# Moving the first weight roundings of a fused attention and MLP kernel: later MLP roundings, a projection piece on VectorE, and three rounds of maxima taken forward

## The chip, the cores and the metric

The kernel runs on one core of a Trainium2 chip. A core has five engines with a queue of their own each: TensorE (PE; its weight loads are shown apart as PEld), VectorE (DVE), ScalarE (ACT), GpSimd (POOL) and SyncE (SP), which here issues nearly all DMAs. The metric is device time in microseconds (us), the median of several executions. All times below on the trace's own clock are us from the start of the profiled span.

## The reference

For x of 2048 tokens by 576 features, the reference gates an attention branch against an MLP branch:

```
g = sigmoid(sum(x * gate_w))                     # one gate per token
q, k, v = split(x @ wqkv)                        # 32 heads of 18 features
a = softmax(q k^T * 18**-0.5) v  @ wo
y = layernorm(x)
b = gelu(y @ w1 + b1) @ w2 + b2                  # 4608 hidden features
out = g * a + (1 - g) * b
```

All inputs and outputs are float32.

## The kernel before

Products are made with operands in a rounded 32-bit form. To keep float32 accuracy each operand is split into a rounded part and a remainder: an engine writes the rounded part (ACT, lines 370, 692, 710, 722, 777), another one subtracts it from the source (POOL or DVE, lines 166, 693, 711, 723, 778), and a product becomes three.

**Projection stage.** The first part of the program (lines 804 to 905) goes through four blocks of 512 tokens (`tb` 0 to 3). Each block has 17 groups `g`: nine of q and k (`qk_group`, 14 products of 512 columns each) and eight of v (`v_group`, 14 products of 288 columns). Between the groups the loop places other work by group number: the normalisation (`norm`, DVE, in block 3 at groups 2 to 5), the transposition of the normalised x (`y_chunk`: four TensorE transposes into a PSUM bank, ACT rounds it, DVE subtracts; in block 3 at groups 8 to 12), loads, and rounds of attention maxima.

**wqkv.** In block 0 the weights arrive in seven pieces (0 to 4 of q and k, 5 and 6 of v), through two buffers in turn. `W_AT` says at which group piece n is split (`split_w`: ACT rounds, the given engine subtracts) and piece n+2 loaded into the buffer that piece n leaves.

**Rounds of maxima.** Softmax takes the maximum of a row first. A round (`s1_round`) is two score products (line 210, one PSUM bank each) and two DVE maxima (line 212). The first unit (one pair of heads, half of the queries) has 32 rounds; `ROUNDS` says how many stand behind each group. When all 32 are done, `s1_finish` (lines 220 to 223, DVE), a transposition on TensorE (line 227), a copy on ACT (229) and two DMAs bring the maxima to the q operand. 40 rounds in all precede the main loop: those that the groups don't hold are made right after the last group, with one `run_due` each. In this stage all products of line 210, the transposes of x and line 227 share the three banks of `ps_s1` in turn, so the fourth waits until the first one's reader is done.

**MLP weights.** The MLP runs as a generator whose steps are interleaved with attention. Its w1 comes in pairs of chunks (one 576 KB load in two DMAs, line 349, into the one buffer `R1`), its w2 in single chunks (line 355, two buffers in turn). `split` puts a job in the list `bg`: ACT rounds (line 370), POOL subtracts (line 166), and then the next load into the buffer is issued. A job may run once the program's step counter `slot` has passed the number in `LOADED`, that is a fixed count of steps behind the load's issue. `run_due` makes such a step; in block 3 `SLOTS` calls it once per group up to group 8 and twice from group 9. The first loads stand at group 2, the first three jobs at group 9, and the second part of the normalised input (`load_y(0, 1)`, six DMAs of 384 KB, line 124) inside group 16, on the SP queue behind that group's store of v (line 802). Everything is recorded in this order, and each engine runs its own queue in order.

**Main loop.** 512 steps of score products (line 250), exponentials (ACT, 253), maxima of the next unit, products with v (268) and pieces of the MLP (454 first layer, 534 second layer). The first MLP products stand in step 1; the first pair has 18 products twice with the first part of the normalised input, and then 18 with its second part (six behind each third of the load).

Of the kernel before, what the change touches and what calls it, by code (L numbers as in the profile page):

```python
# [40 lines left out]
LAND = 8  # L41
# [5 lines left out]
LAST = 28  # L47
PSTEP = (489, 494, 497, 499)
ORDER = (0, 1, 3, 2)
ROUNDS = [lambda g: 0, lambda g: int(g >= 8), lambda g: int(g >= 2), lambda g: int(g >= 5)]  # L50
SLOTS = [lambda g: 0, lambda g: 0, lambda g: int(g >= 4), lambda g: 1 if g < 9 else 2]
SKIP = 0
N_AT = 5
W_AT = {0: 1, 1: 2, 2: 3, 4: 4, 6: 5, 8: 6}
W_CUT = (0, 128, 416, 704, 992, 2 * D, 3 * D - 288, 3 * D)
NSTEP = 512
FIN = NSTEP - 12
# [3 lines left out]
def gated_mix_kernel(ctx: ExitStack, tc: tile.TileContext, x, wqkv, wo, w1, b1, w2, b2, gate_w, out):  # L61
    nc = tc.nc
# [38 lines left out]
    def psum(pool):  # L101
        return pool.tile([P, TB], F32, name="ps")
# [16 lines left out]
    def bcast_rows(ap, n):  # L119
        return bass.AP(tensor=ap.tensor, offset=ap.offset, ap=[[0, P], [1, n]])  # L120
# [6 lines left out]
    slot = [0]  # L127
# [183 lines left out]
    looped = [False]  # L311
# [9 lines left out]
    def mlp():  # L321
# [3 lines left out]
        n = len(seq)  # L325
# [3 lines left out]
        def chunk(q):  # L329

            i, m = divmod(q, G // 2)
            return i, m, seq[i][1] * G + 2 * m
# [5 lines left out]
        LOADED = {}  # L338
        NQ0 = npair // NB

        def load_w1(q):

            if (1, q) in LOADED or q >= NQ0:
                return
            LOADED[1, q] = slot[0] + (LAND if looped[0] else 5)
            fc = chunk(q)[2]
            for h in range(2):
                src = w1[:, (fc + h) * P:(fc + h + 1) * P]
                nc.sync.dma_start(R1[64 * h:64 * h + 64], src.rearrange("(c p) n -> p c n", p=64))

        def load_w2(c):
            if (2, c) in LOADED or c >= NFC:
                return
            LOADED[2, c] = slot[0] + (LAND - 2 if looped[0] else 3)
            nc.sync.dma_start(R2[c % 2], w2[c * P:(c + 1) * P, :])

        def rounded(dst, src):
# [241 lines left out]
        for i in range(n + 1):  # L599
            q = 2 * i  # L600
# [49 lines left out]
    with ExitStack() as a:  # L650
# [17 lines left out]
        def load_x(tb):  # L668

            xt[tb] = x_tile()  # L670
            v = x_view(tb)
            rows = x[tb * TB:(tb + 1) * TB, :].rearrange("(t p) d -> p t d", p=P)
            for c0, c1 in ((0, 256), (256, D)) if tb == 0 else ((0, D),):
                nc.sync.dma_start(v[:, :, c0:c1], rows[:, :, c0:c1])
            nc.sync.dma_start(v[:, :, D:], rows[:, :, 512:D])
# [3 lines left out]
        def load_w(n):  # L679
            cs = slice(W_CUT[n], W_CUT[n + 1])  # L680
            wide = W_CUT[n + 1] - W_CUT[n]
            raw = pp.tile([P, 2, 2, TB], F32, name="p").rearrange("p a b c -> p (a b c)")[:, :5 * wide]
            raw = wraw[n] = raw.rearrange("p (c n) -> p c n", n=wide)
            nc.sync.dma_start(raw[:, 0:4, :], wqkv[0:512, cs].rearrange("(c p) n -> p c n", p=P))
            nc.sync.dma_start(raw[0:64, 4, :], wqkv[512:576, cs])
            nc.sync.dma_start(raw[64:128, 4, :], wqkv[512:576, cs])

        def split_w(n, eng):
            c0 = W_CUT[n] if W_CUT[n] < 2 * D else W_CUT[n] - 2 * D
            hi, lo = [w_[:, :, c0:c0 + W_CUT[n + 1] - W_CUT[n]] for w_ in (W_QK if W_CUT[n] < 2 * D else W_V)]  # L690
            raw = wraw.pop(n)
            nc.scalar.activation(hi, raw, AF.Copy)
            eng.tensor_tensor(lo, raw, hi.bitcast(F32), op=ALU.subtract)  # L693
# [38 lines left out]
        def norm(tb, stage):  # L732

            xv = x_view(tb)
            ts_ = slice(4 * tb, 4 * tb + 4)
            if stage < 2:
                for t in (2 * stage, 2 * stage + 1):
                    st6 = sm.tile([P, 2, nc.vector.BN_STATS_DIM], F32, name="st6")
                    for n in range(2):
                        nc.vector.bn_stats(st6[:, n, :], xv[:, t, n * ND:(n + 1) * ND])  # L740
                    nc.vector.bn_aggr(stats[:, tb * 4 + t, :], st6)
            if stage == 1:
                rstd = rstds[tb] = sm.tile([P, 4], F32, name="rstd")
                sd = sm.tile([P, 4], F32, name="sd")
                var = sm.tile([P, 4], F32, name="var")
                nc.vector.tensor_scalar(var, stats[:, ts_, 1], LN_EPS, None, op0=ALU.add)
                nc.scalar.activation(sd, var, AF.Sqrt)

                nc.vector.reciprocal(rstd, sd)
                nc.vector.tensor_mul(rstd, rstd, var)  # L750
                nc.vector.tensor_add(sd, sd, rstd)
                nc.vector.tensor_scalar(sd, sd, 0.5, None, op0=ALU.mult)
                nc.vector.reciprocal(rstd, sd)
            if stage >= 2:
                junk = pp.tile([P, 2, 2, TB], F32, name="p").rearrange("p a b c -> p (a b c)")
                for t in (2 * stage - 4, 2 * stage - 3):
                    tt = 4 * tb + t
                    nc.vector.scalar_tensor_tensor(junk[:, :D], xv[:, t, 0:D], 1.0, gwb, op0=ALU.mult, op1=ALU.mult,  # L758
                                                   accum_out=glog[:, tt:tt + 1])
                    nc.vector.tensor_scalar(xv[:, t, :], xv[:, t, :], stats[:, tt, 0:1], rstds[tb][:, t:t + 1],  # L760
                                            op0=ALU.subtract, op1=ALU.mult)
# [61 lines left out]
        for tb in range(NB):  # L823
            work = [(qk_group, (tb, mt)) for mt in (range(9) if tb < 2 else (4, 0, 1, 2, 3, 5, 6, 7, 8))] + [(v_group, (tb, t, n)) for t in range(4) for n in range(2)]
            for g, (fn, args) in enumerate(work):
                if tb == 0:
                    if g in W_AT:
                        n = W_AT[g]
                        split_w(n, nc.gpsimd if n > 1 else nc.vector)
                        if n + 2 < 7:  # L830
                            load_w(n + 2)
                    if g == 10:
                        nc.sync.dma_start(b2b, bcast_rows(b2, D))
                        nc.sync.dma_start(b1r, b1.rearrange("(c p) -> c p", p=P))
                if tb == NB - 1 and g == 16:
                    args += (lambda: next(stream[0]),)
                fn(*args)
                ng = g - (N_AT if tb == 0 else 2)
                if 0 <= ng < 4:
                    norm(tb, ng)  # L840
                if tb + 1 < NB and 2 <= g < 7:
                    x_chunk(tb + 1, g - 2)
                yg = g - (11 if tb == 0 else 8)
                if 0 <= yg < 5:
                    y_chunk(tb, yg)
                if g == (16 if tb == 0 else 13) and tb + 2 < NB:
                    load_x(tb + 2)
                if tb == NB - 1:
                    if g == 1:
                        load_k(0, 3 * TB, S)  # L850
                    if g == 2:
                        load_q(1)
                        next(stream[0])
                    if g == 9:
                        qkstack.close()
                        wp1 = mstack.enter_context(tc.tile_pool(name="m_w1", bufs=3))
                        wp2 = mstack.enter_context(tc.tile_pool(name="m_w2", bufs=4))
                        next(stream[0])

                        nc.scalar.activation(gate, glog, AF.Exp, scale=-1.0)  # L860
                    if g == 14:
                        nc.vector.tensor_scalar(gate, gate, 1.0, None, op0=ALU.add)
                        nc.vector.reciprocal(gate, gate)
                        nc.vector.tensor_scalar(gate1, gate, -1.0, 1.0, op0=ALU.mult, op1=ALU.add)
                    if g == 7:
                        ps = psum(ps_s1)
                        nc.tensor.transpose(ps[:, :NFC], b1r, ident[:NFC, :NFC])
                        nc.vector.tensor_copy(b1t, ps[:, :NFC])
                if tb == 1 and g == 5:
                    load_q(0)  # L870
                    load_k(0, 0, TB)
                if tb == 1 and g == 9:
                    load_k(0, TB, 2 * TB)
                if tb == 2 and g == 4:
                    load_k(0, 2 * TB, 3 * TB)
                for _ in range(ROUNDS[tb](g)):
                    next_round()
                for _ in range(SLOTS[tb](g)):
                    run_due()
# [282 lines left out]
```

## Time and profile before

| what | value |
|---|---|
| median of the runs | 2332.59 us (2330.83 to 2334.19, 3 runs) |
| the profiled execution | 2332.71 us |
| its span in the trace | 2330.9 us |
| TensorE busy | 2290.9 us, 98% |
| VectorE, ScalarE, GpSimd busy | 71%, 61%, 42% |
| granted TensorE clock, mean | 0.997 |

The profiled execution lies 0.12 us above the median, and 1.8 us of it lie outside the span. TensorE is busy nearly throughout, so time is lost or won where TensorE stands idle or has half its clock. The projection stage ends at about 244 us; the main loop follows up to about 2210 us, and the last projection behind it.

### The profile page before, as it was taken

The numbers are of one execution on the slowest core, as the hardware profiler recorded it, in microseconds if no ns is written. First come the engines' busy times: TensorE is split into PE (matmuls) and PEld (weight loads), VectorE is DVE, ScalarE is ACT, GpSimd is POOL, SyncE is SP. The second block draws the span as 40 slices with busy tenths as digits, with TensorE's granted clock in tenths as the row PEclk, the third lists the DMA queues.
The fourth block names the chain that finished last, engine by engine and source line by source line (L and its number), as shares of the span: only waits on it lengthen the run. The fifth ranks groups of instructions, "written<-read, shape, count | busy, mean of one in ns | idle before, by whom it ended". The sixth has DMA issues, their size and how long they took to land.

```text
span 2330.9 us, 51536 instructions
## 1 busy us (share of the span) xinstructions
PE 2290.9 (98%) x20585; PEld 1566.0 (67%) x20585; DVE 1654.7 (71%) x2890; ACT 1424.6 (61%) x2629; POOL 968.5 (42%) x965
## 2 busy tenths in 40 slices
PE   8998999999999999999999999999999999999999
PEld 7876666666666666666666666666666666666668
DVE  5675677777777777777777777777777777777734
ACT  4222567777676666666666666666666666666662
POOL 4001566666555433333353444444434333333700
PEclk9999899999999999999999999999999999999999
DMA  7747845445456523343263524242354233242264
GB/s 244 243 151 234 235 163 154 140 145 143 133 189 166 159 96 118 103 135 110 76 172 130 161 95 120 94 138 96 118 162 151 95 107 105 99 147 91 77 213 160
DMA packets 165022, 330.31 MB, mean 142 GB/s; under 512 B 57190, under 2 KB 84490, under 8 KB 154054
## 3 DMA queue, kind: packets, MB, share of 16 engines
q1 hardware_dynamic: 163162, 323.76, 44.2%
q8 instruction: 162, 2.65, 0.5%
q10 hardware_dynamic: 1620, 3.26, 0.4%
q14 instruction: 78, 0.64, 0.1%
HBM read 234.16 MB, written 96.58 MB: 142 GB/s over the span
## 4 chain that ended last, share of the span: by engine, by line
PE 93%; DVE 3%; issue 1%; DMA 1%; SPq 0%; ACT 0%; POOL 0%; ACTq 0%; DVEq 0%; POOLq 0%
PE ps L534 21%; PE ps L268 20%; PE ps L454 20%; PE ps L250 13%; PE ps L210 11%; PE ps L771 3%; PE ps L1058 3%; PE ps L792 2%; DVE m L212 1%; DMA p<-in_A_wqkv_dram 0%; PE ps L698 0%; DVE p L758 0%; DVE x L760 0%; DVE hl L778 0%; PE ps L227 0%
## 5 line engine op out<-in xcount | busy, mean ns | idle before, releaser
L212 DVE TENSOR_REDUCE m<-ps 128x1 f32<-128x512 f32 x2048 | 1317.0, 685 | 460.3 <-PE ps L210 442.8
L253 ACT ACTIVATE p<-ps 128x512 f32<-128x512 f32 x1368 | 742.0, 596 | 404.3 <-PE ps L250 393.0
L166 POOL TENSOR_SCALAR zz<-zz 128x512 f32<-128x512 f32 x288 | 178.5, 620 | 826.0 <-ACT zz L507 796.1
L454 PE MATMUL ps<-big,w 64*128 64x512 f32 x3888 | 513.5, 393 | 0.1
L534 PE MATMUL ps<-w,hh 64*128 64x288 f32 x4352 | 489.9, 299 | 12.5 <-ACT z L475 0.4
L253 ACT ACTIVATE ring<-ps 128x512 f32<-128x512 f32 x680 | 369.1, 596 | 203.0 <-PE ps L250 199.5
L210 PE MATMUL ps<-ka,qa 54*128 54x512 f32 x2048 | 454.6, 415 | 10.3 <-DVE hl L723 5.4
L250 PE MATMUL ps<-qa,ka 56*128 56x512 f32 x2048 | 453.6, 422 | 1.6 <-ACT p L253 1.0
L454 PEld LDWEIGHTS ps<-big,w 64*128 64x128 f32 x3888 | 381.0, 185 | 74.6 <-ACT z L475 0.4
L534 PEld LDWEIGHTS ps<-w,hh 64*128 64x128 f32 x4352 | 383.5, 185 | 68.4 <-issue 45.4
L166 POOL TENSOR_TENSOR zz<-zz,z 128x512 f32<-128x512 f32 x288 | 371.8, 1291 | 24.0
L250 PEld LDWEIGHTS ps<-qa,ka 56*128 56x128 f32 x2048 | 205.1, 184 | 215.1 <-DVE m L212 179.3
L268 PE MATMUL ps<-p,vt 128*32 128x512 f32 x2736 | 344.6, 598 | 0.0
L534 PE MATMUL ps<-w,hl 64*128 64x288 f32 x2176 | 334.2, 292 | 0.0
L210 PEld LDWEIGHTS ps<-ka,qa 54*128 54x128 f32 x2048 | 213.4, 186 | 79.5 <-ACT p L253 25.6
L166 POOL TENSOR_TENSOR w<-x,w 128x576 fp32r<-128x576 f32 (+1 forms) x54 | 98.5, 1839 | 306.1 <-ACT w L370 272.3
L534 PEld LDWEIGHTS ps<-w,hl 64*128 64x128 f32 x2176 | 218.1, 185 | 5.1
L166 POOL TENSOR_TENSOR hl<-zz,hh 128x512 fp32r<-128x512 f32 x136 | 176.7, 1299 | 11.3
L268 PE MATMUL ps<-ring,vt 128*32 128x512 f32 x1360 | 179.1, 598 | 0.0
L268 PEld LDWEIGHTS ps<-p,vt 128*32 128x32 f32 x2736 | 71.4, 109 | 159.4 <-issue 152.1
L543 DVE SCALAR_TENSOR_TENSOR x<-ps,x 128x288 f32<-128x288 f32 x256 | 104.1, 448 | 11.8 <-PE ps L534 11.8
L771 PE MATMUL ps<-big,wqk 128*128 128x512 f32 x432 | 109.7, 402 | 1.4 <-POOL wqk L693 1.4
(100 smaller groups left out, 1368.4 us busy)
## 6 DMA issues: line engine op xcount, KB each, us to landing
w<-w_scr SPq DMA_DIRECT2D x54, 1152.0 KB
w<-w_scr SPq DMA_DIRECT2D x108, 576.0 KB
x<-in_B_w_dram SPq DMA_DIRECT2D x72, 288.0 KB
w_scr<-w SPq DMA_DIRECT2D x18, 1152.0 KB
w_scr<-w SPq DMA_DIRECT2D x36, 576.0 KB
big<-y_scr SPq DMA_DIRECT2D x42, 384.0 KB
qa<-qk_scr SPq DMA_DIRECT2D x192, 72.0 KB
ka<-qk_scr SPq DMA_DIRECT2D x84, 144.0 KB
```

Source lines behind the costliest of these rows:

```text
L166: fn(*args, **kw)
L210: nc.tensor.matmul(ps, qa[r0:r0 + 54, t * P:(t + 1) * P], ka[r0:r0 + 54, kb * TB:(kb + 1) * TB], start=True, stop=True)
L212: nc.vector.tensor_reduce(M4[u][:, h, t, kb:kb + 1], ps, axis=AX.X, op=ALU.max)
L250: nc.tensor.matmul(ps[h], ka[r0:r0 + 56, kc * P:(kc + 1) * P], qa[r0:r0 + 56, qb * TB:(qb + 1) * TB], start=True, stop=True)
L253: nc.scalar.activation(RING[n % 3][:, qb, h], ps[h], AF.Exp, scale=SCALE)
L268: nc.tensor.matmul(OB[u][r:r + 32, :], v[:, k, 19 * h:19 * h + 32], RING[c % 3][:, qb, h, :], start=(k == 0), stop=(k == NT - 1))
L454: nc.tensor.matmul(ps[h], wt[w_][r, c, :], Y[s_][r, c, :], start=(k == 0), stop=(k == 26))
L534: nc.tensor.matmul(ps[nn][:, :ND], h_[r, tok], w_[p_][r, cs[nn]], start=(k == 0), stop=(k == 6 * G - 1))
L543: nc.vector.scalar_tensor_tensor(dst, ps[nn][:, :ND], 0.5, b2b[:, cs[nn]] if g == 0 else dst, op0=ALU.mult, op1=ALU.add)
L771: nc.tensor.matmul(ps, w_[:, c, ms], big[:, s_, :], start=(k == 0), stop=False)
L792: nc.tensor.matmul(ps[:, :ND], big[:, s_, tok], w_[:, c, cs], start=(k == 0), stop=False)
L1058: nc.tensor.matmul(ps[:, :ND], OT[b][2][:, s_, tok], w_part(w_, c)[:, cs], start=(k == 0), stop=(k == 13))
```

## The change

Five edits, all of them to constants that place work:

- `W_AT`: the first piece of v (5) is split at group 5 in place of 6, the second (6) at group 7 in place of 8; the loads that follow a split go with it.
- `split_w` of piece 2 subtracts on VectorE in place of GpSimd.
- `ROUNDS` of block 3: groups 5, 6 and 7 hold two rounds each in place of one, so three of the rounds that stood right before the main loop (four there) move forward. The 32nd round of the first unit then stands at group 9 in place of 12, and its `s1_finish` and the transposition of line 227 move with it, to groups 9 and 10 (line 227 stands right behind group 10's round).
- `LOADED` of w1 and w2 ahead of the main loop: 7 steps in place of 5 and 3.

```
-ROUNDS = [lambda g: 0, lambda g: int(g >= 8), lambda g: int(g >= 2), lambda g: int(g >= 5)]
+ROUNDS = [lambda g: 0, lambda g: int(g >= 8), lambda g: int(g >= 2), lambda g: int(g >= 5) + int(5 <= g < 8)]
...
-W_AT = {0: 1, 1: 2, 2: 3, 4: 4, 6: 5, 8: 6}
+W_AT = {0: 1, 1: 2, 2: 3, 4: 4, 5: 5, 7: 6}
...
-            LOADED[1, q] = slot[0] + (LAND if looped[0] else 5)
+            LOADED[1, q] = slot[0] + (LAND if looped[0] else 7)
...
-            LOADED[2, c] = slot[0] + (LAND - 2 if looped[0] else 3)
+            LOADED[2, c] = slot[0] + (LAND - 2 if looped[0] else 7)
...
-                        split_w(n, nc.gpsimd if n > 1 else nc.vector)
+                        split_w(n, nc.gpsimd if n > 2 else nc.vector)
```

What this does to the queues, engine by engine: the first three MLP roundings on ACT keep their place (group 9). Those of the third and fourth w2 chunk move from between the roundings of the fourth and fifth `y_chunk` to behind the ScalarE copy of group 13's v, where that of the second w1 pair follows them; the third w1 pair's rounding moves from just before the main loop's first exponentials to behind the first four of them. On SP, the load of the third w1 pair still stands one place ahead of group 16's store of v and of `load_y(0, 1)`, and it waits for the subtraction of the second pair, which now comes later; the loads of q and k for the next units move ahead of the first store of a split weight. From the loop's first tens of steps on, the order of the instructions is the same on every engine.

## The prediction

> **What bounds the kernel now.** I read the page first, then windows, then the timelines of the stage that the edits touch.
>
> ```profile
> span 2330.9 us, 51536 instructions
> PE 93%; DVE 3%; issue 1%; DMA 1%; SPq 0%; ACT 0%; POOL 0%; ACTq 0%; DVEq 0%; POOLq 0%
> ```
>
> The chain of waits is 93% TensorE, so the change is worth the idle or half-clock time of TensorE that it takes away, less what it adds. Windows show where that is (columns: length, then busy time of PE, PEld, DVE, ACT, POOL, each with its count, then the granted clock, DMA share, GB/s):
>
> ```profile
> 20.00:40.00 20.00, 18.59 (x91) 14.88 (x90) 9.75 (x22) 9.66 (x13) 11.06 (x4) 1.00 0.83 244
> 220.00:240.00 20.00, 14.03 (x75) 11.26 (x74) 8.85 (x19) 5.00 (x10) 9.82 (x6) 0.83 0.70 233
> 229.20:232.60 3.40, 0.00 (x0) 0.00 (x0) 0.00 (x0) 1.20 (x3) 1.81 (x2) 1.00 0.99 326
> 232.60:239.40 6.80, 5.50 (x19) 4.26 (x19) 4.05 (x10) 1.59 (x3) 3.24 (x2) 0.50 0.51 171
> 246.30:249.70 3.40, 2.79 (x7) 1.02 (x6) 3.40 (x7) 0.40 (x1) 2.62 (x1) 1.00 1.02 259
> 249.70:256.50 6.80, 6.80 (x28) 5.74 (x30) 3.61 (x6) 2.27 (x4) 0.00 (x0) 0.50 1.07 217
> 242.00:244.00 2.00, 2.00 (x16) 1.88 (x14) 1.29 (x2) 0.24 (x1) 0.00 (x0) 1.00 1.13 242
> 247.00:257.00 10.00, 9.50 (x38) 7.08 (x39) 6.36 (x12) 2.47 (x5) 2.40 (x1) 0.66 1.06 225
> ```
>
> TensorE is nearly full except around 228 to 233, and its clock is halved twice, for 6.8 us each: after it stood idle, and after a stretch (246.3 to 249.7) of seven products only. An episode costs at most 6.8 / 2 = 3.4 us.
>
> **Step 1, the front.** Piece 2 and the v pieces end two waits.
>
> ```profile
> 22.64 2.60 PE L771 MATMUL ps<-big,wqk 128*128 128x512 f32 x10 [1.41 <-POOL wqk L693]
> 46.85 1.71 PE L792 MATMUL ps<-wv,big 128*128 128x288 f32 x11 [1.05 <-POOL wv L693]
> 17.76 1.41 ACT L692 ACTIVATE wqk<-p 128x1440 fp32r<-128x1440 f32 x1 [3.54 <-DMA p<-in_A_wqkv_dram]
> 12.28 1.66 DVE L693 TENSOR_TENSOR wqk<-p,wqk 128x1440 fp32r<-128x1440 f32 x1 [0.65 <-ACT wqk L692]
> 41.39 0.58 ACT L777 ACTIVATE hh<-ps 128x512 fp32r<-128x512 f32 x1
> ```
>
> Piece 2 is rounded at 19.2; a subtraction of its size takes 1.66 on DVE, so it is there at 20.9, before TensorE asks at 21.2: -1.4. On DVE the splits of groups 1 and 2 queue behind it, 1.7 us later at most, and behind those only SP's stores of q and k; no product waits for them, so this costs nothing while the buffers of those splits (six) last. SP's load of piece 4 waits for this subtraction and goes out sooner, and POOL has one job less. The last v piece's rounding now stands ahead of the copy at 41.39, 0.5 sooner; its chain and TensorE both shift by the 1.4, so the 1.05 wait shrinks by 0.5. Sum -1.9 (bounds -1.4 and -2.5, both waits gone).
>
> **Step 2, two rounds behind groups 5 to 7.** This is the change's price.
>
> ```profile
> 198.11 0.50 PE L210 MATMUL ps<-ka,qa 54*128 54x512 f32 x2
> 198.55 3.06 PE L771 MATMUL ps<-big,wqk 128*128 128x512 f32 x12
> 202.77 1.28 DVE L212 TENSOR_REDUCE m<-ps 128x1 f32<-128x512 f32 x2
> 203.51 0.50 PE L210 MATMUL ps<-ka,qa 54*128 54x512 f32 x1 [1.00 <-DVE m L212]
> 203.94 3.07 PE L771 MATMUL ps<-big,wqk 128*128 128x512 f32 x12
> 207.08 0.39 PE L774 MATMUL ps<-big,wqk 128*128 128x512 f32 x1
> 207.90 3.06 PE L771 MATMUL ps<-big,wqk 128*128 128x512 f32 x12
> 208.90 1.28 DVE L212 TENSOR_REDUCE m<-ps 128x1 f32<-128x512 f32 x2
> ```
>
> DVE is in the normalisation until 202.8. The first maximum ends at 203.4, and the fourth product since 198.1 (now group 6's second) waits for it to 203.51. With four products behind group 5 the fourth is theirs: TensorE idles from about 199.0 (three products of 0.22 and their drain) to 203.5. Queued behind it are group 6's fourteen products, and behind those ScalarE's copy, DVE's split and two stores on SP. Group 6 starts at 203.94, not 198.55: +5.4. Behind groups 6 and 7 the fourth product waits for that group's split and one maximum: from the end at 207.4 to 208.90 + 0.64 is 2.1, against about 0.9 for three products, 1.2 idle each. Group 8 starts at 203.94 + 2 x (3.45 + 2.1 + 0.2) = 215.4, not 207.90: +7.5. If DVE's normalisation were done sooner the 5.4 would shrink to the 1.2 of the others; nothing in the edits moves it, so the bounds are +5 and +8.
>
> **Step 3, the clock after that gap.** 4.5 us of idle stand between the two known cases, idle from 227.9 to 233.35 and the seven-product stretch, which both halved the clock. Half clock for 6.8 us falls on the one dense group of 3.4 us, which then takes up to twice as long, and partly on the next 1.2 wait, which hides some: I take +2.6, near the 5.50 busy us of 232.6 to 239.4, half of which was lost (2.75). Bounds 0 (no halving) and 3.4.
>
> **Step 4, line 227 earlier.** It takes the bank of the third normalised chunk, whose rounding stands behind the first MLP jobs.
>
> ```profile
> 215.00 0.66 PE L698 MATMUL ps<-ident,x 128*128 128x128 f32 x4 [0.65 <-DVE hl L723]
> 217.72 2.29 ACT L370 ACTIVATE w<-x 128x1152 fp32r<-128x1152 f32 x3
> 220.53 0.69 DVE L723 TENSOR_TENSOR hl<-ps,hh 128x512 fp32r<-128x512 f32 x1 [1.31 <-ACT hh L722]
> 222.01 0.97 PE L210 MATMUL ps<-ka,qa 54*128 54x512 f32 x2
> ```
>
> That bank is free 6.3 us behind the second chunk's transposes (215.0 to 221.2); TensorE would be there after 3.9: +2.35. Gone are the 0.65, about 0.6 in the round behind it, and 0.45 at 222.01, which came of a late ScalarE. Net +0.6 (bounds -1.7 and +2.4). Queued behind line 227 is group 11. The finish's four small DVE instructions, the copy on ScalarE and two DMAs on SP move too; the DMAs now stand ahead of the fourth w2 chunk's load and delay it by their issue, which step 5's later rounding covers.
>
> **Step 5, the roundings behind their loads.**
>
> ```profile
> 228.42 0.68 ACT L370 ACTIVATE w<-x 128x576 fp32r<-128x576 f32 x1 [5.70 <-DMA x<-in_B_w_dram]
> 231.40 0.68 ACT L370 ACTIVATE w<-x 128x576 fp32r<-128x576 f32 x1 [2.30 <-DMA x<-in_B_w_dram]
> 233.35 1.39 PE L210 MATMUL ps<-ka,qa 54*128 54x512 f32 x2 [5.41 <-DVE hl L723]
> 235.29 0.39 PE L227 MATMUL ps<-ident,nm 128*32 128x128 f32 x1 [0.56 <-DVE nm L223]
> ```
>
> ScalarE stood at two roundings for their loads, with the last chunk's rounding queued behind, for whose bank TensorE waited. These now stand behind group 13's copy, with no bank of TensorE behind them. So 5.4 and line 227's 0.6 go, and with the idle window the first half-clock stretch: half of its 5.50 busy us, 2.7. Sum -8.7 (bounds -6, the stretch staying, and -8.7).
>
> **Step 6, the rounds ahead of the loop.**
>
> ```profile
> 244.13 0.73 PE L210 MATMUL ps<-ka,qa 54*128 54x512 f32 x3
> 245.41 4.09 PE L210 MATMUL ps<-ka,qa 54*128 54x512 f32 x7 [0.55 <-DVE m L212]
> 249.59 1.39 PE L250 MATMUL ps<-qa,ka 56*128 56x512 f32 x2
> 252.26 4.21 PE L454 MATMUL ps<-big,w 64*128 64x512 f32 x18
> 256.76 2.36 PE L454 MATMUL ps<-big,w 64*128 64x512 f32 x18
> 259.32 2.35 PE L454 MATMUL ps<-big,w 64*128 64x512 f32 x18
> ```
>
> Six of ten products at DVE's pace of 0.6 go: -3.6. The thin stretch shrinks to some 2 us, so the second halving may go too: 4.21 against 2.36, and 0.6 around it, -2.5.
>
> Group 16 then ends at 244.1 - 1.9 + 7.5 + 2.6 + 0.6 - 8.7 = 244.2, as now, and the third eighteen of line 454, which end at 261.7 today, could end at about 255.7: 1.9 for four products at DVE's pace, then today's 12.1 from 249.59 less 2.5, is 11.5 behind it. That is -6.
>
> **Step 7, what is late next.** Those eighteen need the second part of the normalised input.
>
> ```profile
> 237.12 2.65 POOL L166 TENSOR_TENSOR w<-x,w 128x1152 fp32r<-128x1152 f32 x1 [3.56 <-ACT w L370]
> 239.99 1.39 SPq L349 DMA_DIRECT2D x<-in_B_w_dram  x2
> 245.18 3.87 SPq L124 DMA_DIRECT2D big<-y_scr  x6
> ```
>
> It is 6 x 384 KB = 2.36 MB; at the 217 to 225 GB/s of the windows above that is some 10.7 us, to about 257.3, 2 us ahead of its use. It starts on group 16, so it doesn't get sooner. It gets later: the third w1 pair's load, issued at 239.99 when POOL has the second pair done, had 5 us before the input's six DMAs were issued. Now POOL ends near group 16's end. Counted from the second chunk's transposes (215.0 today), group 13 ends after 12.9 - 0.6 - 0.45 + 2.35 = 14.2, and group 16 after three more rounds and v groups of some 2.4 each, 21.4. The first moved rounding can start 0.4 behind group 13's end, at 14.6, is done 0.7 later, and POOL needs 2 x 1.4 (half of a 2.65, as half of the elements) + 2.65: 20.8, or 21.3 if a load is late. So SP issues that load just ahead of the input's six DMAs, and its 0.59 MB at 242 GB/s lie in front: +2.4, less a small overlap, +2.0 (bounds 0 and 3.5). The input is complete at 257.3 + 0.1 + 2.0 = 259.4, six products follow, 0.8: 260.2 against 261.7. ScalarE's and DVE's first-layer bias, and POOL's chain for GELU, queue behind it and shift alike. **Sum -1.5 to -1.6** against the profiled execution's 2332.71, which is 0.1 above the median: 2331.1, on the median's scale 2331.0. Of the -6, 4.4 is lost to this wait. Behind it the orders agree. The fourth w1 pair's load moves behind the loads of q and k on SP; its rounding has over 10 us of slack today and I cost it at nothing, but it would cap a larger gain.
>
> **The clock, weighed.** The trace halves the clock after 3.4 us with seven products, each 0.22 us by the pace of the pair at 198.11: at most 45% in use, and no gap as long as 0.6. [...] The row of 246.3 shows that less than full idleness is enough. [...]
>
> **The rivals.** *The input arrives in time* (faster): POOL's jobs run before group 15, the load is not in the way, and the group-5 gap misses the clock. Then -6 - 2.6 = -8.6 at best; the start on group 16 caps it, with 10.7 us of transfer, near -5 to -6: 2327.0. For it: 2 us of slack today; against it: the queue order. *More half-clock stretches* (slower): today there are two. The gap at group 5, that at line 227 (2.35) and the wait for the input would be three; each is 3.4 at most, the first is counted. One more gives +1.8, 2334.4; both +5.2, 2337.8. It decides from the second extra one. For it speaks the row of 246.3; against it, that no gap there is as long as the 5.4 of today, and that the rest around line 227 is dense. *The wait only moves*: the two w2 loads land after group 13's copy too, POOL slips and with it the loads: each us of slip costs one, 2 to 4: 2333 to 2335.
>
> **How the numbers follow.** A measurement here can tell about 0.2%, 4.7 us. Forecast as summed 0.42 (its own range 2328.5 to 2334); input in time 0.22; one extra stretch 0.17, both 0.13; wait moved 0.06. Faster takes the rival's 0.22 and a little of the forecast's tail: 0.23; slower the 0.13 and tails: 0.19; within, 0.58. The range 2326 to 2338 reaches to both rivals.
>
> **What would show it.** Right: no wait at the third group's products nor at 228 to 233; an idle gap of 4 to 5 us behind group 5, then half clock; 2 us at line 227; a wait inside the third eighteen of line 454 on the load of the input. Wrong: no gap at group 5 (step 2 is the largest loss), the input's load complete before those products, or a load for a ScalarE rounding still waited for in front of a normalised chunk.

## The result and the profile after

The changed kernel takes 2342.75 us (median of 5 runs, 2342.35 to 2346.0) against 2333.21 us before (5 runs, 2330.83 to 2335.61): a ratio of 1.0044 with an interval of 1.0030 to 1.0057. It is slower by 0.4%, where 2331.0 us in a range of 2326 to 2338 was forecast. The same kernel measured again (run 15 below) gave 1.0044 once more (1.0031 to 1.0058).

The profiled execution of the changed kernel took 2346.0 us, 3.2 above its median, so its trace shows somewhat more than the typical loss. First the page's span and its chain of waits; then, in one list, windows of 20 us (columns as in the prediction) and the windows in which the granted clock is 0.50:

```profile
span 2344.2 us, 51541 instructions
...
PE 94%; DVE 3%; DMA 1%; issue 1%; ACT 1%; SPq 0%; ACTq 0%; DVEq 0%
```

```profile
200.00:220.00 20.00, 14.16 (x38) 9.41 (x38) 9.80 (x19) 1.19 (x2) 0.00 (x0) 0.74 0.92 232
220.00:240.00 20.00, 17.73 (x102) 14.67 (x101) 11.00 (x22) 7.87 (x14) 5.37 (x3) 0.91 0.49 165
240.00:260.00 20.00, 17.36 (x88) 13.74 (x88) 15.09 (x22) 6.71 (x11) 6.17 (x4) 0.84 0.84 245
260.00:280.00 20.00, 15.37 (x102) 10.34 (x101) 5.86 (x10) 6.74 (x13) 7.21 (x7) 0.82 0.91 171
202.51:209.34 6.83, 6.07 (x14) 4.47 (x15) 2.50 (x5) 0.00 (x0) 0.00 (x0) 0.50 1.06 202
212.75:216.16 3.41, 3.41 (x9) 2.63 (x8) 0.99 (x2) 0.00 (x0) 0.00 (x0) 0.50 1.03 392
233.23:236.64 3.41, 3.41 (x16) 3.09 (x14) 0.52 (x1) 0.42 (x1) 2.42 (x2) 0.50 0.44 121
250.30:253.71 3.41, 3.41 (x16) 3.02 (x14) 1.29 (x3) 0.00 (x0) 0.00 (x0) 0.50 0.79 169
257.12:260.54 3.42, 3.42 (x16) 3.42 (x18) 1.90 (x4) 2.03 (x3) 1.31 (x1) 0.50 1.06 218
270.78:277.60 6.82, 5.46 (x25) 2.05 (x26) 2.15 (x4) 3.10 (x7) 3.78 (x4) 0.50 0.62 142
1721.44:1724.86 3.42, 3.42 (x28) 3.26 (x30) 1.29 (x2) 1.64 (x4) 3.04 (x4) 0.50 0.84 173
```

The kernel before had two half-clock stretches of 6.8 us each ahead of the loop's steady part; this one has six there and one in the loop. At a clock of 0.50, a stretch loses at most half of TensorE's busy time in it. Before, that is (5.50 + 6.80) / 2 = 6.2 us; now (6.07 + 3.41 + 3.41 + 3.41 + 3.42 + 5.46) / 2 = 12.6, and 1.7 in the loop. So at most 6.4 us ahead of the loop's steady part, and 8.1 with the stretch in the loop, of the 13.3 that this execution is longer are the clock's.

**Group 5 to group 8.** TensorE's timeline:

```profile
203.27 0.79 PE L210 MATMUL ps<-ka,qa 54*128 54x512 f32 x1 [4.67 <-DVE m L212]
203.99 5.48 PE L771 MATMUL ps<-big,wqk 128*128 128x512 f32 x12
...
212.00 0.50 PE L210 MATMUL ps<-ka,qa 54*128 54x512 f32 x1 [1.40 <-DVE m L212]
212.43 4.61 PE L771 MATMUL ps<-big,wqk 128*128 128x512 f32 x12
...
219.07 1.10 PE L210 MATMUL ps<-ka,qa 54*128 54x512 f32 x2 [1.07 <-DVE b1t L868]
220.10 3.06 PE L771 MATMUL ps<-big,wqk 128*128 128x512 f32 x12
```

The three waits (4.67, 1.40 and 1.07) stand where they were forecast. A group's twelve products take 3.06 at full clock; those of groups 6 and 7 take 5.48 and 4.61. Group 8 starts at 220.10 in place of 207.90.

**Line 227, and the gate beside GpSimd.** First TensorE at line 227; then rows of ScalarE, GpSimd, VectorE and TensorE around group 14, each from its engine's timeline (lines 862 to 864 finish the token gate `g` of the reference):

```profile
232.61 0.28 PE L227 MATMUL ps<-ident,nm 128*32 128x128 f32 x1 [2.27 <-DVE hl L723]
232.65 2.76 PE L792 MATMUL ps<-wv,big 128*128 128x288 f32 x12
```

```profile
243.40 1.74 ACT L370 ACTIVATE w<-x 128x576 fp32r<-128x576 f32 x2 [0.17 <-DMA x<-in_B_w_dram]
...
243.31 5.40 POOL L166 TENSOR_TENSOR w<-x,w 128x576 fp32r<-128x576 f32 x3 [7.66 <-ACT w L370]
...
245.05 1.11 DVE L862 TENSOR_SCALAR gate<-gate 128x16 f32<-128x16 f32 x1
...
246.49 2.26 DVE L864 TENSOR_SCALAR gate<-gate 128x16 f32<-128x16 f32 x1
...
249.39 0.49 PE L210 MATMUL ps<-ka,qa 54*128 54x512 f32 x1 [1.84 <-DVE m L212]
249.81 2.88 PE L792 MATMUL ps<-wv,big 128*128 128x288 f32 x12
```

The roundings find their data (0.17 of wait in place of 5.70). But GpSimd's three subtractions now run from 243.31 to 248.71, and two VectorE operations on 16 columns take 1.11 and 2.26 us; the second ends at 248.75, with the last subtraction. The maxima queued behind them are late: TensorE has a new wait of 1.84, and half clock behind it (250.30 to 253.71).

**From group 16 on.** TensorE, and the SP queue:

```profile
255.24 1.10 PE L250 MATMUL ps<-qa,ka 56*128 56x512 f32 x2
...
257.56 3.73 PE L454 MATMUL ps<-big,w 64*128 64x512 f32 x18
...
267.24 0.49 PE L454 MATMUL ps<-big,w 64*128 64x512 f32 x1 [1.51 <-DMA big<-y_scr]
269.49 0.96 PE L454 MATMUL ps<-big,w 64*128 64x512 f32 x5 [1.76 <-DMA big<-y_scr]
...
272.28 3.64 PE L268 MATMUL ps<-p,vt 128*32 128x512 f32 x16 [1.36 <-DMA vt<-v_scr]
```

```profile
248.74 1.38 SPq L349 DMA_DIRECT2D x<-in_B_w_dram  x2
...
254.15 3.88 SPq L124 DMA_DIRECT2D big<-y_scr  x6
```

The load of the third w1 pair (line 349) goes out 5.4 us ahead of the input's (line 124), and the third eighteen products of line 454 wait for the input, 3.3 us in two gaps. The products with v then wait 1.36 for a load queued behind the input, and run at half clock. They start at 272.28; in the kernel before, on its timeline, at 262.06:

```profile
262.06 1.92 PE L268 MATMUL ps<-p,vt 128*32 128x512 f32 x16
```

So 10.2 of this execution's 13.3 us are lost up to that point, and 3.1 behind it; of these the stretches from 270.78 and 1721.44 hold at most 2.7 and 1.7.

### The profile page after: what moved, and what is told of

It is laid out like the page before. It is cut to its first block, busy times and chain, and to the rows that moved or that the text cites. A ratio compares the mean times of both kernels' runs of the same rounds, so it can differ in the third digit from the quotient of the medians.

```text
span 2344.2 us, 51541 instructions
## 1 busy us (share of the span) xinstructions
PE 2297.0 (98%) x20585; PEld 1570.1 (67%) x20585; DVE 1658.1 (71%) x2891; ACT 1424.2 (61%) x2629; POOL 964.9 (41%) x964
## 4 chain that ended last, share of the span: by engine, by line
PE 94%; DVE 3%; DMA 1%; issue 1%; ACT 1%; SPq 0%; ACTq 0%; DVEq 0%
PE ps L534 21%; PE ps L268 20%; PE ps L454 19%; PE ps L250 13%; PE ps L210 11%; PE ps L771 4%; PE ps L1058 3%; PE ps L792 2%; DVE m L212 1%; DMA vt<-v_scr 1%; PE ps L698 1%; DVE p L758 0%; PE ps L774 0%; DVE hl L778 0%; PE ps L773 0%
## 5 line engine op out<-in xcount | busy, mean ns | idle before, releaser
L543 DVE SCALAR_TENSOR_TENSOR x<-ps,x 128x288 f32<-128x288 f32 x256 | 104.1, 448 | 12.6 <-PE ps L534 12.6
```

The costliest lines, as they stand in the source:

```text
L543: nc.vector.scalar_tensor_tensor(dst, ps[nn][:, :ND], 0.5, b2b[:, cs[nn]] if g == 0 else dst, op0=ALU.mult, op1=ALU.add)
```

## The experiments

Medians are in us, ratios against the kernel before on the same chip; the brackets and the column "interval" hold 95% intervals of the ratio. The front edits are `W_AT` and the engine of piece 2; the roundings' edit is the two counts of 7.

**1 to 4: the parts.** Each is the kernel before with one or two of the edits.

```
1  ROUNDS:  + int(5 <= g < 8)
2  LOADED:  w1 5 -> 7, w2 3 -> 7
3  W_AT: {..., 5: 5, 7: 6};  nc.gpsimd if n > 2 else nc.vector
4  2 and 3 together
```

> Only the rounds' edit is made to the kernel before (two rounds behind groups 5 to 7; line 227 goes earlier with it). Theory A, the clock's: the wait behind group 5 (about 4.7 us) and the shorter waits behind it cost their idle time and about twice a half-clock stretch, so group 8 starts about 12 us later than the kernel before's 207.90; 3.4 us come back ahead of the main loop, because three rounds fewer stand there; the waits at 228 to 233 for the w2 loads stay or shrink as the loads gain time. The kernel before plus 5 to 10 us: 2338 to 2343. Rival, the prediction's sum for these steps: +7.5 + 2.6 + 0.6 - 3.6 - 2.5 = +4.6, less what of the load wait the delay hides: 2334 to 2338. A time at or below 2333 would clear the rounds.

> Only the two counts of steps are raised to 7 in the kernel before; rounds, pieces of wqkv and their engines stay. Theory A: the wait of 5.4 us at 233.35 and the half-clock stretch behind it go (-8), and 0 to 5 us of it are given back where GpSimd's subtractions now run beside VectorE's gate operations at group 14 and where the input's second part is late: 2325 to 2330. Rival B, the later roundings themselves carry the loss (GpSimd beside VectorE, then late maxima, another half-clock stretch, and the load of the third w1 pair in front of the input): at or above 2333. The trace tells them apart at 240 to 270 us: B needs VectorE's instructions of line 862 and 864 at 1 to 2 us each and a half-clock stretch there.

> Only the projection's weights are changed: third piece subtracted on VectorE, the v pieces one group sooner. By the traces of before and after, group 5's first maxima come 0.24 us sooner, no more: the kernel before less 0.2, 2333. The prediction's step 1 says -1.9: 2331.3. A row of ScalarE's rounding of the first v piece with a wait for its load of about 3 us is the mark of the former.

> The changed kernel with the rounds of the kernel before, that is e2_loaded and e3_front together. Theory A (the rounds are the whole loss): as e2_loaded within 1 us, 2325 to 2330, and the difference from the changed kernel is that of the rounds with their clock, 12 to 17 us. Rival: the later roundings lose in any case, 2333 or more, and the rounds cost under 10.

| run | median | ratio | interval |
|---|---|---|---|
| 1, rounds | 2345.81 | 1.0055 | 1.0040 to 1.0070 |
| 2, roundings | 2327.67 | 0.9977 | 0.9968 to 0.9987 |
| 3, front | 2332.16 | 0.9995 | 0.9986 to 1.0005 |
| 4, front and roundings | 2325.80 | 0.9970 | 0.9958 to 0.9981 |

The rounds are the whole loss: 0.55% alone, and 0.74% on top of the other two edits (1.0044 against 0.9970), 12 and 17 us; the first figure is above the range of both theories, which end at 2343. One reason why they cost less alone is that the wait which came of the w2 loads, 5.41 in the kernel before, is 3.71 in the first run's trace: the later start hides part of it. The roundings bring 6 us, as theory A said. The fourth run is faster than both kernels.

The front brings 1 to 2 us by these medians; the third run's interval takes in no change. How much, hangs on the load of the first v piece. ScalarE's rounding of it in the third and fourth run and in the changed kernel, each from its own timeline:

```profile
31.05 1.41 ACT L692 ACTIVATE wv<-p 128x1440 fp32r<-128x1440 f32 x1 [2.16 <-DMA p<-in_A_wqkv_dram]
```

```profile
29.77 1.41 ACT L692 ACTIVATE wv<-p 128x1440 fp32r<-128x1440 f32 x1 [0.88 <-DMA p<-in_A_wqkv_dram]
```

```profile
32.04 1.41 ACT L692 ACTIVATE wv<-p 128x1440 fp32r<-128x1440 f32 x1 [3.25 <-DMA p<-in_A_wqkv_dram]
...
45.68 1.72 PE L792 MATMUL ps<-wv,big 128*128 128x288 f32 x11 [1.64 <-POOL wv L693]
```

Group 5's first round of block 3 stands at 196.92, 196.73 and 197.87 in these three, against 198.11 before: 1.2, 1.4 and 0.2 sooner, for waits of 2.16, 0.88 and 3.25. In the changed kernel the v wait grew from 1.05 to 1.64 in place of shrinking by 0.5. Over the fifteen traces with the front edits ScalarE's wait is 0.87 to 3.33 and that round stands at 196.67 to 198.27, so a comparison of two single traces can carry 1 us or more of this. Both traces of the changed kernel have a wait above 3.2; those of runs 5, 7, 13 and 16 have 0.95 to 1.25.

**5: the clock at groups 5 to 7.** Unused products fill the three gaps; the waits and all orders stay.

```
+SPARE = {5: (0, 18), 6: (0, 5), 7: (4, 0)}
...
+        for _ in range(n):
+            nc.tensor.matmul(ps, W_QK[0][:, 0, 0:P], xT[NB - 1][:, 0, :], start=True, stop=True)
```

> The changed kernel with 27 products more, whose results are not used: 18, 5 and 4 of them (0.23 us each, written into the bank of the next group's sums, which that group starts afresh) stand on TensorE right ahead of the product that waits behind groups 5, 6 and 7. They fill the gaps of 4.67, 1.40 and 1.07 us and delay nothing. Theory A, the clock's: the two half-clock stretches at 202 to 216 go, group 6's twelve products take 3.06 in place of 5.48 and group 7's 3.06 in place of 4.61, so 4.0 us come back: 2338 to 2339.5. Rival: the idle time itself is the loss and the clock follows no gap: 2342 to 2343. A share of 4 us that is lost again further on (later groups meet the loads earlier) would show as a longer wait at 233 to 270.

Measured 2339.71 (1.0027; 1.0016 to 1.0038): 3.0 below the changed kernel's median and 0.2 above theory A's range, nearer to the clock's 4.0 than to nothing, though the two intervals still touch. Its TensorE timeline (line 208 is the unused products, 222 the rounds', 783 the groups'):

```profile
197.55 4.46 PE L208 MATMUL ps<-big,wqk 128*128 128x512 f32 x18
202.29 0.50 PE L222 MATMUL ps<-ka,qa 54*128 54x512 f32 x1 [0.27 <-DVE m L224]
202.72 3.06 PE L783 MATMUL ps<-big,wqk 128*128 128x512 f32 x12
...
208.73 3.07 PE L783 MATMUL ps<-big,wqk 128*128 128x512 f32 x12
```

The same wait for the same maximum, 27 products more, and the twelve products of groups 6 and 7 are back at 3.06 and 3.07. This trace shows the cause more directly than the time does.

**6: one round behind group 5.**

```
-int(g >= 5) + int(5 <= g < 8)
+int(g >= 5) + int(6 <= g < 8)
```

> The changed kernel with one round behind group 5 and two behind groups 6 and 7 only; one round more stands ahead of the loop. Theory A: the gap of 4.67 behind group 5 shrinks to today's 1.0 and the half-clock stretch of 6.8 behind it goes, so group 8 starts 5 to 8 us sooner than in the changed kernel, the additional round ahead of the loop costs 1.2: 2335 to 2338. Rival: the loss is carried by everything behind group 8 (line 227, late maxima, the input) and only 1 to 3 us come back: 2340 to 2342.

Measured 2335.10 (1.0008; 0.9999 to 1.0017), in theory A's range: 7.65 us of the loss hang on the second round behind group 5. The 9 us that remain above the fourth run go with the rounds behind groups 6 and 7: in this trace group 6's twelve products still take 4.38, line 227 waits 2.12, and the wait behind the gate is 1.85.

**7: the gate away from GpSimd.**

```
-                    if g == 14:
+                    if g == 11:
```

> The changed kernel with VectorE's three gate operations (lines 862 to 864) moved from group 14 to group 11, away from GpSimd's three subtractions at 243 to 249. Theory A: beside GpSimd these operations take 1.11 and 2.26 us in place of 0.34 and 0.17, and the maxima behind them are late for that: the wait of 1.84 at 249.39 and the half clock behind it go, group 16 ends 2.5 to 3.5 us sooner and the input with it: 2339 to 2340.5. Rival: the maxima are late for another reason, or the input's wait takes it all: 2342 to 2343.

Measured 2340.84 (1.0035; 1.0021 to 1.0049), 1.9 below the changed kernel: between the two theories. Its VectorE timeline:

```profile
236.72 0.17 DVE L862 TENSOR_SCALAR gate<-gate 128x16 f32<-128x16 f32 x1
...
237.21 0.17 DVE L864 TENSOR_SCALAR gate<-gate 128x16 f32<-128x16 f32 x1
```

With GpSimd idle (its jobs end near 234.4 and begin again at 242.3) they take 0.17 each, and the wait of 1.84 at this place is down to 0.56. Of the 3.0 us that the two slow operations cost VectorE, some 2 reached the end by the medians; the two intervals overlap, so that size is not shown.

**8 and 9: what stands ahead of the input.** Both are the fourth run with one count changed.

```
8  LOADED w1: 7 -> 5
9  LOADED w2: 7 -> 13
```

> The kernel of the fourth experiment (the change without the rounds) with the count of w1 back at 5 and that of w2 at 7: the second w1 pair is then rounded and subtracted some 3 us earlier, so that the load of the third pair (0.59 MB, about 4 us of the DMA engines just ahead of the input) goes out earlier. Theory A (prediction's step 7: that load stands in front of the input): the input's last part lands about 3 us sooner, its wait of 1.52 in front of the third eighteen of line 454 goes: 2324.0 to 2325.0. Rival: the input is bound by its own 10 us and by the store of v, or its wait only turns into another one: 2325.5 to 2327.

> The kernel of the fourth experiment (the change without the rounds) with the count of w2 at 13 in place of 7: the third and fourth w2 chunk are rounded behind group 16, so the two w2 loads that follow them (0.59 MB together) are issued behind the input's six DMAs, and only the third w1 pair's load is left in front. Theory A: the input waits for whatever the queue holds in front of it (the eighth run changed one 0.59 MB for another and its wait only went from 1.52 to 0.89): its last part lands 2 us sooner, no wait is left in the third eighteen of line 454: 2324 to 2325. Rival: the input is bound by the end of group 16 and its own transfer, 2325.5 to 2327.

The eighth run took 2328.77 (0.9979; 0.9970 to 0.9988), the ninth 2325.20 (0.9967; 0.9955 to 0.9979). The eighth missed: its wait was 0.89 in place of 1.52, and it was no faster. Its trace also has the first v piece late (3.33 of wait against 0.88 in the fourth's), so it doesn't settle what the wait is worth. In the ninth the third eighteen runs without a wait, and the products with v start at 253.13 against 255.05 in the fourth's trace; in the time the two can't be told apart.

**10: the three rounds at groups 13 to 15,** on the ninth.

```
-int(g >= 5)
+int(g >= 5) + int(13 <= g < 16)
```

> As the ninth run, and the three rounds taken from ahead of the loop stand behind groups 13, 14 and 15 (v groups, no normalised chunk left, VectorE half idle) in place of groups 5 to 7. Theory A: the loss of the change lies in where the rounds went, not in moving them: behind each of the three groups a wait of 0.5 to 0.8 for one maximum, +2; ahead of the loop -3.6, and the half-clock stretch of 6.8 us at 240 goes, -3: 2320 to 2323. Rival: two rounds in any group cost a half-clock stretch, as at groups 5 to 7, or the input caps the gain: 2325 to 2329.

Measured 2334.19 (1.0010; 1.0001 to 1.0019): missed by 11 us or more, and slower than the rival. VectorE and TensorE of its timeline:

```profile
230.55 2.02 DVE L862 TENSOR_SCALAR gate<-gate 128x16 f32<-128x16 f32 x1
...
233.72 0.50 PE L210 MATMUL ps<-ka,qa 54*128 54x512 f32 x1 [2.92 <-DVE m L212]
...
258.91 1.51 PE L454 MATMUL ps<-big,w 64*128 64x512 f32 x5 [1.63 <-DMA big<-y_scr]
```

```profile
232.57 1.35 SPq L349 DMA_DIRECT2D x<-in_B_w_dram  x2
...
243.61 3.88 SPq L124 DMA_DIRECT2D big<-y_scr  x6
```

The gate met GpSimd's subtraction again, so that with four products behind a group the wait was 2.92, and half clock followed it. The run therefore doesn't tell a round at these groups from that meeting. It does tell something on the input: the last weight load ahead of it was issued 11 us earlier, and still it took 258.91 - 243.61 = 15.3 us from its issue to its last part's use, as in the changed kernel (269.49 - 254.15 = 15.3), where the third pair's load was issued 5.4 ahead. Over the thirteen traces that show this wait it is 13.9 to 16.9: 15.9 to 16.9 in the five with a weight load issued 1.6 to 2.2 us ahead (runs 2, 4, 7, 8 and 11), 13.9 to 15.3 in the eight where it went out 3.5 us ahead or more. So a load right in front goes with 1 to 2 us more, but most of the time is the input's without it.

**11: line 227 late,** in the changed kernel.

```
-                defer(1, lambda: s1_finish(u))
+                defer(7 if u == 0 else 1, lambda: s1_finish(u))
```

> The changed kernel with the finish of the first unit's maxima put off, so that line 227 stands behind group 12's round as in the kernel before. Theory A: in the changed kernel its wait of 2.27 at 232.61 and the half clock of 3.4 us behind it cost some 3 us and bring nothing: 2339 to 2340.5. Rival (the prediction's step 4: net +0.6, since other waits come back when it is gone): 2342 to 2343.

Measured 2339.10 (1.0028; 1.0018 to 1.0038), 3.65 below the changed kernel, with intervals that overlap a little: line 227's new place costs a wait of 2.3 and the half clock behind it. In this run's trace line 227 waits 0.32, and there is no half clock behind it.

**12 and 14: the clock ahead of the loop.** The ninth run with one unused product behind each product of the last four rounds, in two shapes.

```
12  nc.tensor.matmul(KEEP[0], ka[:, 0:P], ka[:, 0:TB], start=True, stop=True)
14  nc.tensor.matmul(KEEP[0], qa[0:54, ...], ka[0:54, ...], start=True, stop=True)
```

> The kernel of the ninth run with eight products more, whose results are not used: one behind each product of the four rounds ahead of the loop, into the bank of the first products with v, which is free there. TensorE is then busy for some 0.46 of each 0.6 us in place of 0.23. Theory A, the clock's: the half-clock stretch of 10.2 us that the ninth run shows from 237.6 goes, of which some 3.5 us of products were lost (4.21 in place of 2.3 in the first eighteen of line 454 alone), and the input, complete near 248, now caps part of it: 2321.5 to 2323.5. Rival: the stretch there costs nothing, since the input or the exponentials end last: 2324.5 to 2326.

> As the twelfth run, with the unused products in the shape of the rounds' own (54 rows in place of 128). The twelfth run's took 0.43 us of TensorE's time each where two shapes alternate, which stretched the rounds from 5.5 to 8.0 us; in one shape a product takes 0.23. Theory A: the rounds keep VectorE's pace of 0.6 and the half-clock stretch of 10.2 us that begins with them goes: 2321.5 to 2323.5. Rival: the stretch is not on the path, or the pace suffers again: 2324.5 to 2327.

Theory A missed in both: 2327.65 (0.9973; 0.9962 to 0.9985), above the rival's range too, and 2324.72 (0.9960; 0.9947 to 0.9972), in the rival's range. In the twelfth a product took TensorE 0.43 us where the two shapes alternate, at full clock (its record is 0.50 long there, and 0.79 in the half-clock stretch behind), so a pair took 0.86 and VectorE waited for products:

```profile
241.67 0.69 DVE L215 TENSOR_REDUCE m<-ps 128x1 f32<-128x512 f32 x1 [0.17 <-PE ps L211]
242.53 0.69 DVE L215 TENSOR_REDUCE m<-ps 128x1 f32<-128x512 f32 x1 [0.17 <-PE ps L211]
```

The half-clock stretch came in both, 6.8 us from 243.5 in the twelfth and, though the pace of 0.6 was kept there, from 243.8 in the fourteenth. In the twelfth the profile shows TensorE busy throughout the 3.4 us ahead of it (240.12 to 243.54), with 9 products: there the half clock came without a gap, and the products that filled it did not keep it away. The fourteenth's gain against the ninth lies within both intervals; whether that stretch is on the path stays open. The fourteenth has the lowest median of all, but the intervals don't tell it from the fourth run, which needs no unused products.

**13, 15 and 16: the clock everywhere ahead of the loop.** The thirteenth is the changed kernel with unused products at groups 5 to 7, ahead of line 227 (9), in group 15's round (7), and, as in the twelfth, ahead of the loop; the sixteenth is the same kernel again. The fifteenth is the changed kernel again, on the sixteenth's chip.

```
+SPARE = {5: (0, 18), 6: (0, 5), 7: (4, 0), 15: (0, 7)}
...
+            if u == 0:
+                spare(9)
```

> The changed kernel with unused products in all its gaps ahead of the loop: the 27 of the fifth run, 9 ahead of line 227, 7 ahead of the second product of group 15's round, and one behind each product of the round ahead of the loop. All waits stay, only the clock is kept up; the wait for the input keeps its halving. Theory A: of the changed kernel's loss against the kernel before (+9.5) the clock's share is 3 at groups 5 to 7, about 1 at line 227, 1.5 at group 15: 2336 to 2338. Rival: past group 8 the clock's loss is hidden by the wait for the input, so that nothing is left beyond the fifth run's 3.0: 2339.5 to 2341.

> The changed kernel itself again, on the chip of the thirteenth run's repeat, for a second trace of it. Its first products with v stood at 272.3 us in the first trace, against 262.1 in the kernel before: +10.2 of its loss lie ahead of the loop. Theory A: again 270 to 273, and the loop as long as the others' (2068 to 2073 us): 2341 to 2345. Rival: that trace was one of the slow executions and the typical loss ahead of the loop is smaller: 266 to 269.

> The thirteenth run's kernel again (unused products in all gaps ahead of the loop). Its trace had the first products with v at 262.2, as the kernel before (262.1), but a loop of 2076.3 us against 2068 to 2073 in the others, with an idle time of 1.6 us and a half-clock stretch near 2261. Theory A: 262 to 264 again, and that loop was a chance of the execution: 2333 to 2336 for executions without it. Rival: the loop belongs to this kernel: again 2337 to 2340 with a loop of 2074 or more.

| run | median | ratio | interval |
|---|---|---|---|
| changed kernel | 2342.75 | 1.0044 | 1.0030 to 1.0057 |
| 15, the same again | 2345.72 | 1.0044 | 1.0031 to 1.0058 |
| 13, gaps filled | 2338.74 | 1.0018 | 1.0009 to 1.0027 |
| 16, the same again | 2336.37 | 1.0009 | 1.0000 to 1.0019 |

The first products with v in the fifteenth and sixteenth run (line 285 is line 268 there):

```profile
271.07 3.64 PE L268 MATMUL ps<-p,vt 128*32 128x512 f32 x16 [0.79 <-DMA vt<-v_scr]
```

```profile
263.07 2.71 PE L285 MATMUL ps<-p,vt 128*32 128x512 f32 x16 [0.27 <-DMA vt<-v_scr]
```

With the clock kept up nearly everywhere (one stretch is left, at the input) and the waits left in, the changed kernel reaches this point at 263.07 (262.2 in the thirteenth), within 1 us of the kernel before (262.06); without, at 272.28 and 271.07. Of these 8 to 10 us, 0.9 to 1.0 are the first v piece's load, as group 5's first round shows (196.83 against 197.87 and 197.76). So the half clock that was filled away is worth 7 to 9 us up to this point, and 0.26% to 0.35% by the times, 6 to 8 us. That is the changed kernel's whole half clock but one stretch, not the difference from the kernel before, which has two stretches of its own (6.2 us at most) and was not run filled. The waits are therefore not free: without any half clock the changed kernel would only draw level with a kernel before that keeps its own.

The thirteenth missed both ranges (2338.74 between 2338 and 2339.5); the sixteenth came to 263.07 as theory A said, with a time 0.4 above its range, and the fifteenth to 271.07, with a time 0.7 above. The loop of the filled kernel was longer than the kernel before's (2076.3 and 2071.9 us of the span lie behind that point, against 2068.8). Part of the thirteenth's is a wait for ScalarE and half clock near 2261, which the sixteenth doesn't have. The changed kernel's own two traces have 2071.9 and 2074.1 there, with most of the stretch at the products with v and the one in the loop; how much of the 3 to 5 us these explain stays open.

## Why the prediction was wrong

The waits that were forecast came where they were forecast. What failed above all is the price of the clock behind them (step 3). Besides, two gains that were counted did not come in full (steps 1 and 4), and two waits were not forecast: 1.84 behind the gate and 1.36 for v.

**Step 1 failed in part.** Piece 2's wait went, -1.4. "The last v piece's rounding now stands ahead of the copy, 0.5 sooner" did not hold: the first v piece's rounding stands at group 5, its load was not there, and ScalarE waited 3.25 with a copy queued behind it. Group 5 gained 0.24, not 1.9. Moving a rounding towards its load is the mistake that the change repairs elsewhere; the prediction did not look for it here.

**Step 2 was right.** Group 6 at 203.94 forecast, 203.99 measured; the waits behind groups 6 and 7 were 1.40 and 1.07 for 1.2. Group 8 was forecast at 215.4 at full clock; it came at 220.10, and without the 4.0 of half clock on groups 6 and 7 it would be 216.1.

**Step 3 is the term that was mis-sized.** One stretch for +2.6 (bounds 0 and 3.4) was forecast; two came, on groups 6 and 7, and cost 2.4 + 1.55 by their twelve products. Behind it the rest of the sum took the clock as full: line 227, group 15, the first eighteen of the first layer and the products with v each had a stretch that the sum had at nothing or had as gone. In the sum the clock's part was +2.6, less 2.7 and most of step 6's 2.5 for the two stretches of the kernel before, about -2; by the windows it is up to +6.4 ahead of the loop and 1.7 in it. That is at most 8 to 10 of the 11.75 us between forecast and median, on a trace 3.2 above the median. The filled runs give a smaller figure: they take 6 to 8 us of half clock out of the changed kernel, where the sum had left 2.6 in it, 3.5 to 5.5 too little, and they still hold one stretch. The rest of the 11.75 stands in the other steps; how it divides among them is not shown.

**The clock, weighed.** The forecast of -1.6 let the wait for the input stay at full clock, which was the author's estimate and stood on no row of the trace before; one stretch more made it +1.8. The trace shows 0.50 behind that wait (270.78 to 277.60). Of the six windows of 3.41 us, the length of the shortest stretches, that lie right ahead of a stretch in that stage, only one was empty, the first of these three:

```profile
199.10:202.51 3.41, 0.00 (x0) 0.00 (x0) 3.34 (x8) 0.00 (x0) 0.00 (x0) 1.00 1.07 199
229.82:233.23 3.41, 1.14 (x8) 0.81 (x8) 2.16 (x7) 2.28 (x5) 2.95 (x2) 1.00 0.02 7
253.71:257.12 3.41, 2.61 (x11) 0.94 (x8) 3.16 (x6) 1.24 (x3) 0.00 (x0) 1.00 0.75 238
```

Behind the last two, with 8 and 11 products, the clock was halved as behind the empty one, and so it was behind the row of seven products in the kernel before. The sum priced one new stretch, at group 5; the waits at line 227 and behind the gate, and the thin stretch at the loop's start, had a stretch behind them as well.

**Step 4** had the wait right (2.27 for 2.35). Its net of +0.6 did not hold: by the medians the eleventh run gives 3.65. "The rest around line 227 is dense" was the reason for no half clock there, but the window from 229.82 has 8 products in 3.4 us.

**Step 5** was right in its cause: the waits for the loads went, and alone the edit brings 5.9 of the 8.7. Not foreseen was that the moved subtractions meet the gate: 1.11 and 2.26 beside GpSimd against 0.17 without, the second ending with GpSimd's last subtraction. Why they take longer beside it is not shown.

**Step 6** came out for the rounds (line 250 starts 2.1 us behind group 16's end, 5.5 before) and not for its halving, which stayed: 3.73 for the first eighteen, against 4.21 before and 2.36 at full clock.

**Step 7** had the place and nearly the size of the wait (3.3 for 4.4). The load in front as its main cause was not borne out: the input takes 13.9 to 15.3 us from its issue where no load stands right in front, and 1 to 2 more where one does. The 10.7 us of "2.36 MB at 217 to 225 GB/s" were too few, and from the issue at 245.18 they end at 255.9, not at 257.3, for which no source is given; the wait for the load behind it (1.36, line 268) was missed.

Of the rivals, *more half-clock stretches* is what came. Its bound of 2337.8 was too low: it counted three places, and the changed kernel's traces show seven stretches, one of them in the loop.

## What to carry to other kernels

Price a new wait on TensorE by what the clock does in the windows behind it, for each wait in turn: here filling the gaps, with every wait left in, took the time from 1.0044 to 1.0018 and 1.0009 of the kernel before's. Such unused products separate idle time from the clock in one run, where they do keep the clock up: in the twelfth and fourteenth run they did not. Compare first whether the two traces start alike: a load ahead of the stage moved these by up to 1.6 us. Work moved to a free engine has to be checked against what runs beside it there (here two VectorE operations of 0.17 that took 1.11 and 2.26), not only for its queue.

## What was not expected of the hardware

- The clock was halved after windows of 3.4 us with 8 products and a gap of 2.27 us, and with 11 products and no gap over 0.6; the stretches lasted 3.4 or 6.8 us (10.2 in the ninth run). The count of products doesn't decide alone: ten from 216.16 to 219.57 were not followed by one. Nor does busy time: in the twelfth run a window of 3.4 us that the profile shows busy throughout, with 9 products, was followed by one.
- A VectorE operation on 128 x 16 took 2.26 us beside a GpSimd subtraction in the changed kernel, and 0.17 without one in the seventh run.
- Products of two shapes in turn (54 rows and 128) took 0.43 us each at full clock in the twelfth run; the fifth run's unused products, all of 128 rows, 0.25 (18 in 4.46).
